# Block sums moved later, the keys' running sum queued behind the key's low part, transposed tiles in PSUM, a split query pass

## The chip, the cores and the metric

The kernel runs on one core of a Trainium2 chip. The metric is device time in microseconds for one whole execution, all inputs and outputs in device memory. Engines named below: TensorE (PE in the profile; PEld is its weight load), VectorE (DVE), ScalarE (ACT), GpSimd (POOL), SyncE (SP), which issues every DMA of this kernel. Each engine works through its own instructions strictly in the order in which the program lists them.

## The reference

Two kinds of layer alternate, A, B, A, B, on a sequence of 2048 tokens of width 512, all in fp32:

```python
def A(x):                                   # 32 heads of 16
    q, k, v = split(layernorm(x) @ wqkv)
    phi = lambda t: where(t > 0, t + 1, exp(t)) + 1e-6
    kv  = einsum("shd,she->hde", phi(k), v);  z = sum_s phi(k)
    o   = einsum("qhd,hde->qhe", phi(q), kv) / (einsum("qhd,hd->qh", phi(q), z) + 1e-6)
    return x + o @ wo
def B(x):                                   # 896 + 896 features
    z  = gelu(layernorm(x) @ w_in);  z1, z2 = z[:, :896], layernorm(z[:, 896:])
    return x + (z1 * (w_sp @ z2 + b_sp)) @ w_out      # w_sp is 2048 x 2048
```

## The kernel before

Tokens are worked in 16 tiles of 128 (NT = 16). Every large product is made of three fp32r matmuls (`mm3`): each operand is written as a high part (ScalarE copy, `high`, line 119) and a low remainder (VectorE subtraction, `low`, line 122), and high x high, high x low, low x high are added up in one PSUM bank. The third matmul (line 135) needs the low part of its first operand, the second (line 134) that of its second. Scratch memory is handed out from first-in-first-out lists: 22 `pages` of 128x512, 6 `quads`, 4 `bigs`, and the 8 PSUM `banks`. Whoever takes a slot waits until its last user is done. The order of all instructions is written out by hand.

One round (L = 0, 1) is one A layer and one B layer, in three stages:

**P1** (keys, queries). `P1.run` has steps s = 1..17. A step makes `T_high(s)`/`T_low(s)` (high and low part of the transposed, normalised tile s), `K(s-1)` and its feature map `K_phi`, `Q(s-1)` and `Q_phi` (only for the first 10 tiles), `xsplit`, `K_split(s-1)` (ScalarE line 340, VectorE line 341, then GpSimd adds the keys to their running sum `zacc`, line 346), and `Gmm(s-2)`, which accumulates x^T phi(k) in four banks. Its second matmul needs the low part from line 341. The transposition goes through memory: ScalarE writes the normalised tile, SyncE stores and reloads it, VectorE transposes 32x32 blocks (line 260, class `Turn`). The pass over `win2`, the weight of the second half of B's first product, is split into its two parts one piece at a time (`side`), from step 7 on. A step with `Q` holds 36 matmuls, a later one 24.

**P2** and `transition` before it. The last six query tiles (`later`) are projected late: one in P1's last step, three in `transition` and two in P2's steps 1 and 2 (`late`); `late_phi` then applies phi: ScalarE lines 327 and 328 (relu, exp), VectorE line 329. P2's step s has `c(s-1)` (attention output, 12 matmuls), `c2` (residual add line 614 and statistics on VectorE, then three small GpSimd instructions, lines 200 to 203), `b_high`/`b_low` (parts of the turned query tile, which `c` of the next step needs), `c3` (normalise on ScalarE, store), `d_high`/`d_low` (parts of the turned tile, which `e` needs), `e(s-3)`, `e2`, `e3` (second half of B's first product, gelu, statistics) and up to two `f` (first half).

**P4** (the 2048 x 2048 product). It is one level of a Strassen-like scheme of seven products over blocks of w_sp, in the order P2, P1, P6, P7, P4, P5, P3 (names of products here, not of stages), eight steps each, g = 0..55. The sums of blocks that P6, P7, P5 and P3 need (s[2], s[3], s[1], s[4]) are made once, by class `Sums`, during round L = 0: a `tick` stores the last sums, loads three blocks or one, and has GpSimd add two pairs (line 782). 32 ticks have work and the 33rd only stores. Step g of P4 does `fetch(g+4)` (loads the operand), `sp(g+2)` (splits it, lines 840, 841, and z, lines 870 to 874), `mm(g)` and, after a product, `evac` with the `gate` multiplications on GpSimd (line 929). After P4 comes the output product `o(i)` for 16 tiles, 21 matmuls each, with `zsplit(i+2)` ahead; in it `join` prepares the next round's P1: at i = 8 and 10 the loads of the key and query weight, at i = 10..13 their splitting, at 14 and 15 the first two turned tiles.

In the kernel before, the ticks are spread so: four in P1 of round 0 (steps 2 to 5, on sheets cut out of two `bigs` by class `Sheets`), 13 in P2 (steps 6 to 18), 16 in P4 (g = 0..15).

Of the kernel before, what the change touches and what calls it, by code (L numbers as in the profile page):

```python
# [29 lines left out]
class Slots:  # L30


    def __init__(self, pool, prefix, n):
        self.pool, self.prefix = pool, prefix
        self.free_list = deque(range(n))
        self.held = {}
        self.count = 0
# [12 lines left out]
            self.free_list.append(n)  # L50


class Sheets:


    def __init__(self, slots, n):
        self.slots = slots
        self.tiles = [slots.get([P, NF, 512]) for _ in range(n)]
        self.free_list = deque(t[:, f, :] for t in self.tiles for f in range(NF))

    def get(self, shape):
        return self.free_list.popleft()

    def put(self, *sheets):
        self.free_list.extend(sheets)

    def close(self):
        self.slots.put(*self.tiles)


@with_exitstack
def mixer_kernel(ctx: ExitStack, tc: tile.TileContext, x_in, wqkv, wo_d, win1_d, win2_d, wsp_d, bsp_d, wout_d,
                 ident_d, mask_d, out_d):
# [39 lines left out]
    def load(ap, slots=pages):  # L113
        t = slots.get(PAGE)
        nc.sync.dma_start(t, ap)
        return t

    def high(h, src):
        nc.scalar.activation(h, src, AF.Copy)  # L119
# [104 lines left out]
    class Turn:  # L224

        def __init__(self, name, by_pe, always=False):
            self.name, self.by_pe, self.always = name, by_pe, always
            self.held, self.d, self.raw = {}, {}, {}  # L230

        def turned(self, i):
# [18 lines left out]
        def get(self, i):  # L251
            if i in self.held:
                s = self.held.pop(i)
                b = transposes(s)
                if self.always:
                    pages.put(s)
                return b, banks
            r = self.raw.pop(i)
            y = pages.get([P, 4, P])
            nc.vector.transpose(y.rearrange("p c (t m) -> p m c t", m=4), r.rearrange("p (m c j) -> p m c j", m=4, c=4))  # L260
            pages.put(r)
            return y, pages


    class P1:
        def __init__(self, L):
            self.L = L
            self.st = 2 * L
            self.x, self.ms, self.xT, self.pk, self.kb, self.r, self.xhl = {}, {}, {}, {}, {}, {}, {}
            self.wk, self.wq = w_square(wqkv, 512), w_square(wqkv, 0, True)  # L270
            self.win2 = w_in2()
            self.later = deque(range(NT - DEFER, NT))
            self.turn = Turn(f"xt{L}", range(3) if L == 0 else ())
            self.G = None
            self.zacc = None

        def loadx(self, i):
            if i < NT:
# [45 lines left out]
            self.kb[i] = self.proj(i, self.wk)  # L324

        def phi(self, b, r):
            nc.scalar.activation(r, b, AF.Relu, scale=-1.0)  # L327
            nc.scalar.activation(r, r, AF.Exp, scale=-1.0)  # L328
            nc.vector.scalar_tensor_tensor(r, b, 0.0, r, op0=OP.max, op1=OP.add)  # L329
            banks.put(b)  # L330

# [5 lines left out]
        def K_split(self, i):  # L337
            r = self.r.pop(i)
            h, l = pages.get(PAGE, F32R), pages.get(PAGE, F32R)
            nc.scalar.activation(h, r, AF.Copy, bias=PHI_EPS)  # L340
            nc.vector.scalar_tensor_tensor(l, r, PHI_EPS, h.bitcast(F32), op0=OP.add, op1=OP.subtract)  # L341
            self.pk[i] = (h, l)
            if i == 0:
                self.zacc = r
            else:
                nc.gpsimd.tensor_tensor(self.zacc, self.zacc, r, op=OP.add)
                pages.put(r)

        def Q(self, i):
# [14 lines left out]
                    self.wq.free()  # L364

        def late_phi(self):
            if self.later:
                self.Q_phi(self.later.popleft())

        def xsplit(self, i):  # L370
            h, l = pages.get(PAGE, F32R), pages.get(PAGE, F32R)
# [57 lines left out]
        def run(self, sums):  # L429
            side = deque([self.win2] * NF)  # L430
            ND = NT - DEFER
            for s in range(1, NT + 2):
                self.loadx(s + 3)
                self.turn.load(s + 1)
                if 2 <= s < NT:
                    self.T_high(s)
                if s == 1:
                    if not self.kb:
                        self.K(0)
                    self.K(1)  # L440
                elif 2 < s <= NT:
                    self.K(s - 1)
                self.ln_a(s + 2)
                if 2 <= s < NT:
                    self.T_low(s)
                if s <= NT:
                    self.K_phi(s - 1)
                if s <= ND:
                    self.Q(s - 1)
                if s == NT + 1:  # L450
                    self.late()
                if s <= NT:
                    self.xsplit(s - 1)
                    self.K_split(s - 1)
                self.ln_b(s + 2)
                if s <= ND:
                    self.Q_phi(s - 1)
                if s >= 2:
                    self.Gmm(s - 2)
                if s == NT + 1:  # L460
                    self.late_phi()
                if self.L == 0 and s == 2:
                    sums.slots = Sheets(bigs, 2)
                if self.L == 0 and 2 <= s < 6:
                    sums.tick(s < 5)
                if self.L == 0 and s == 6:
                    sums.store()
                    sums.slots.close()
                    sums.slots = pages
                if s == 6:  # L470
                    self.wv, self.wo = (quads.get([P, 4, 512]) for _ in range(2))
                    nc.sync.dma_start(self.wv, wqkv[:, 1024:1536].rearrange("(c p) f -> p c f", p=P))
                    nc.sync.dma_start(self.wo, wo_d.rearrange("(c p) f -> p c f", p=P))
                if s > 6 and side:
                    side.popleft().piece()
                if s > 5 and side:
                    side[0].fetch()


    def transition(p1, p2):  # L480
# [55 lines left out]
        p1.late()  # L536
        p2.a(3)
        p2.a2(2)
        p1.late_phi()


    class P2:
# [152 lines left out]
        def run(self, sums):  # L695
            w1 = self.win1
            for s in range(1, NT + 3):
                self.loadx(s + 1)
                self.qturn.load(s + 1)
                if s in self.qturn.by_pe:  # L700
                    self.c(s - 1)
                    self.b_high(s)
                    self.c2(s - 1)
                    self.b_low(s)
                    if s >= 2:
                        self.d_high(s - 2)
                        self.d_low(s - 2)
                    self.p1.late()
                    self.c3(s - 1)
                    self.a2(s + 2)  # L710
                    self.p1.late_phi()
                    self.a(s + 3)
                else:
                    if s < NT:
                        self.b_high(s)
                    self.a2_den(s + 2)
                    if s < NT:
                        self.b_low(s)
                    if s <= NT:
                        self.c(s - 1)  # L720
                        self.c2(s - 1)
                    if s == NT:
                        quads.put(*self.W2)
                        pages.put(self.zbc)
                    self.a2_mul(s + 2)
                    late = s - 2 in self.xturn.by_pe
                    if late:
                        self.d_high(s - 2)
                        self.d_low(s - 2)
                    if s <= NT:  # L730
                        self.c3(s - 1)
                    self.a(s + 3)
                    if s <= NT + 1 and not late:
                        self.d_high(s - 2)
                        self.d_low(s - 2)
                if s >= 4:
                    self.e4(s - 4)
                self.xturn.load(s - 1)
                if s >= 3:
                    self.e(s - 3)  # L740
                    self.e2(s - 3)
                    self.e3(s - 3)
                self.f()
                self.f()
                self.fq.extend(self.fnext)
                self.fnext = []
                w1.piece(True)
                w1.fetch()
                if s > 5:
                    sums.tick()  # L750
                if s >= NT + 1:
                    self.p4.fetch(s - NT - 1)
            self.e4(NT - 1)
            self.win2.free()
# [51 lines left out]
    class P4:  # L806
# [197 lines left out]
        def run(self, nxt):  # L1004
# [10 lines left out]
            for g in range(n):  # L1015
# [6 lines left out]
                if evac_first:  # L1022
                    self.evac(p)
                    self.sp(g + 2)
                if g < 16:
                    self.sums.tick()
                if g == 3:
                    self.loadb()
# [21 lines left out]
        def join(self, i, nxt):  # L1050
# [10 lines left out]
                nxt.turn.load(i - 11)  # L1061
            if 10 <= i < 14:
                nxt.wk.piece()
                nxt.wq.piece()
            if i == 14:
                nxt.T(0)
# [48 lines left out]
```

## Time and profile before

| what | value |
|---|---|
| device time, median of 3 runs | 1405.52 us (1405.52 to 1405.92) |
| the profiled execution's own time | 1404.73 us |
| its span, first to last instruction | 1402.9 us |
| granted TensorE clock | 1.000 |
| busy: PE, DVE, ACT, POOL | 1389.6, 886.4, 561.0, 405.6 us |
| DMA traffic | 225.69 MB, 161 GB/s on average |

A row of the views has the start and the duration (us) or, for groups, the count and the mean duration of one instruction (ns); in brackets stands how long the engine was idle before it and what ended that. "pg", "qd", "bg", "bank" are the four kinds of slots; "x<-y" means that x is written from y. A matmul's end is modelled, so that the busy time of TensorE overlaps: what counts is the distance from one start to the next.

### The profile page before, as it was taken

What the parts mean: (1) busy time and instruction counts of PE and PEld (TensorE: products, weight loads), DVE (VectorE), ACT (ScalarE), POOL (GpSimd) and SP (SyncE); (2) the same over time, 40 slices, a digit from 0 to 9 for tenths busy, and PEclk for the clock granted to TensorE, in tenths of its full rate; (3) what the DMA queues carried; (4) which work ended last, traced back from release to release, by engine and by line L of the source; (5) the groups of instructions that cost most, each with busy time, mean ns of one, the idle gap of its engine ahead of it and who ended that gap; (6) DMA issues with size and microseconds to landing.
All of it is one profiled execution on the core that took longest, in us unless ns stands there. A gap on an engine that the chain in (4) does not pass through costs nothing.

```text
span 1402.9 us, 17320 instructions
## 1 busy us (share of the span) xinstructions
PE 1389.6 (99%) x6230; PEld 1156.7 (82%) x6230; DVE 886.4 (63%) x1251; ACT 561.0 (40%) x847; POOL 405.6 (29%) x490
## 2 busy tenths in 40 slices
PE   9999999999999999999999999999999999999998
PEld 7877788888888888888788778888888888888887
DVE  7786777752577666573577867766415466665632
ACT  5564534434323332341356645444333233333420
POOL 4644345544365002040023434432100030022300
PEclk9999999999999999999999999999999999999999
DMA  5842267876897433443635413555334344334432
GB/s 176 270 142 62 73 192 237 271 228 207 305 326 248 134 120 135 173 158 120 210 101 184 129 46 99 179 179 162 114 116 158 104 165 134 133 117 167 155 110 94
DMA packets 142263, 225.69 MB, mean 161 GB/s; under 512 B 11744, under 2 KB 50400, under 8 KB 142176
## 3 DMA queue, kind: packets, MB, share of 16 engines
q1 hardware_dynamic: 142176, 224.57, 48.6%
q8 instruction: 49, 0.80, 0.2%
q14 instruction: 38, 0.31, 0.1%
HBM read 156.63 MB, written 67.90 MB: 160 GB/s over the span
## 4 chain that ended last, share of the span: by engine, by line
PE 87%; DVE 6%; ACT 4%; issue 1%; DMA 1%; POOL 0%; SPq 0%; DVEq 0%; ACTq 0%; POOLq 0%
PE bank L135 15%; PE bank L134 15%; PE bank L133 15%; PE bank L902 13%; PE bank L904 13%; PE bank L903 13%; DVE pg L260 1%; DVE pg L341 1%; DVE pg L329 1%; ACT pg L328 1%; DMA pg<-in_win_dram 1%; ACT pg L327 1%; PE bank L515 1%; PE bank L526 0%; PE bank L221 0%
## 5 line engine op out<-in xcount | busy, mean ns | idle before, releaser
L902 PE MATMUL bank<-qd,pg 128*128 128x512 f32 x800 | 311.2, 389 | 0.0
L904 PE MATMUL bank<-qd,pg 128*128 128x512 f32 x800 | 311.2, 389 | 0.0
L903 PE MATMUL bank<-qd,pg 128*128 128x512 f32 x800 | 311.2, 389 | 0.0
L841 DVE TENSOR_TENSOR qd<-qd,qd 128x1024 fp32r<-128x1024 f32 x112 | 151.8, 1355 | 178.7 <-ACT qd L840 174.2
L840 ACT ACTIVATE qd<-qd 128x1024 fp32r<-128x1024 f32 x112 | 118.5, 1058 | 215.7 <-PE bank L904 199.0
L929 POOL TENSOR_TENSOR bg<-bg,pg 128x512 f32<-128x512 f32 x56 | 85.5, 1564 | 409.7 <-DVE bg L956 195.5
L904 PEld LDWEIGHTS bank<-qd,pg 128*128 128x128 f32 x800 | 150.2, 188 | 31.3
L903 PEld LDWEIGHTS bank<-qd,pg 128*128 128x128 f32 x800 | 150.2, 188 | 31.2
L902 PEld LDWEIGHTS bank<-qd,pg 128*128 128x128 f32 x800 | 150.1, 188 | 31.1
L135 PE MATMUL bank<-qd,pg 128*128 128x512 f32 x384 | 150.7, 392 | 2.5 <-DVE pg L122 2.5
L200 POOL TENSOR_SCALAR rs<-mv 128x1 f32<-128x1 f32 x96 | 36.4, 379 | 384.4 <-DVE mv L198 377.2
L209 ACT ACTIVATE pg<-pg,nb,rs 128x512 f32<-128x512 f32 x63 | 51.1, 811 | 181.6 <-POOL nb L203 175.5
L133 PE MATMUL bank<-qd,pg 128*128 128x512 f32 x288 | 112.4, 390 | 0.0
L134 PE MATMUL bank<-qd,pg 128*128 128x512 f32 x288 | 112.3, 390 | 0.0
L782 POOL TENSOR_TENSOR pg<-pg,pg 128x512 f32<-128x512 f32 x56 | 81.5, 1456 | 47.7 <-DMA pg<-in_wsp_dram 41.8
L133 PE MATMUL bank<-bg,qd 128*128 128x448 f32 x256 | 94.1, 368 | 0.0
L135 PE MATMUL bank<-bg,qd 128*128 128x448 f32 x256 | 93.7, 366 | 0.1
L134 PE MATMUL bank<-bg,qd 128*128 128x448 f32 x256 | 93.6, 366 | 0.0
L135 PEld LDWEIGHTS bank<-qd,pg 128*128 128x128 f32 x384 | 72.0, 188 | 20.8 <-DVE pg L122 6.0
L135 PE MATMUL bank<-wo,qd 128*128 128x512 f32 x224 | 87.3, 390 | 0.8 <-DVE qd L122 0.8
L133 PE MATMUL bank<-wo,qd 128*128 128x512 f32 x224 | 87.3, 390 | 0.7 <-ACT qd L119 0.7
L135 PE MATMUL bank<-qd,bg 128*128 128x512 f32 x224 | 87.4, 390 | 0.0
(121 smaller groups left out, 2571.7 us busy)
## 6 DMA issues: line engine op xcount, KB each, us to landing
qd<-s SPq DMA_DIRECT2D x64, 512.0 KB, 3.4
qd<-in_wsp_dram SPq DMA_DIRECT2D x48, 512.0 KB, 3.8
pg<-x SPq DMA_DIRECT2D x64, 256.0 KB, 2.9
z<-pg SPq DMA_DIRECT2D x56, 256.0 KB, 2.5
pg<-in_wsp_dram SPq DMA_DIRECT2D x56, 256.0 KB, 5.0
s<-pg SPq DMA_DIRECT2D x56, 256.0 KB, 4.8
pg<-z SPq DMA_DIRECT2D x56, 256.0 KB, 5.4
x<-pg SPq DMA_DIRECT2D x48, 256.0 KB, 2.6
```

The costliest lines, as they stand in the source:

```text
L133: nc.tensor.matmul(out, ah, bh, start=start, stop=False)
L134: nc.tensor.matmul(out, ah, bl, start=False, stop=False)
L135: nc.tensor.matmul(out, al, bh, start=False, stop=stop)
L200: nc.gpsimd.tensor_scalar(rs, mv[:, 1:2], LN_EPS, None, op0=OP.add)
L209: nc.scalar.activation(y, x, AF.Identity, bias=nb, scale=rs)
L782: nc.gpsimd.tensor_tensor(t, a, b, op=OP.add)
L840: nc.scalar.activation(w[:, 0], r, AF.Copy)
L841: nc.vector.tensor_sub(w[:, 1], r, w[:, 0].bitcast(F32))
L902: m(out, h[:, o], w[:, 0, j, :], start=start, stop=False, skip_group_check=True)
L903: m(out, h[:, o], w[:, 1, j, :], start=False, stop=False, skip_group_check=True)
L904: m(out, l[:, o], w[:, 0, j, :], start=False, stop=stop, skip_group_check=True)
L929: nc.gpsimd.tensor_tensor(u, u, z1, op=OP.mult)
```

## The change

Seven edits:

1. Class `Sheets` and P1's ticks go. The ticks now run from P2's step 5 (14 of them, one more than before) to P4's g = 18 (19, three more); all their blocks lie in pages.
2. `win2` is split from P1's step 4 on (loaded from step 3 on), instead of step 7 (6).
3. `behind`: GpSimd's add to `zacc` (line 346) waits for the VectorE instruction of line 341 in the same `K_split`.
4. P1's reloaded tiles are transposed into a PSUM bank instead of a page (`inbank`); lines 119 and 122 then read the bank.
5. `late_phi` is cut in two. For the last call in `transition` and those in P2, the ScalarE half stays where it was, and the VectorE half (line 329) goes behind `c2` of the next step, ahead of `b_low`.
6. In `join` the query weight is split at i = 11..14 instead of 10..13.
7. P4's `tick` bound goes from g < 16 to g < 19 (with edit 1).

```diff
--- before.py
+++ after.py
@@ -50,24 +50,6 @@
             self.free_list.append(n)
 
 
-class Sheets:
-
-
-    def __init__(self, slots, n):
-        self.slots = slots
-        self.tiles = [slots.get([P, NF, 512]) for _ in range(n)]
-        self.free_list = deque(t[:, f, :] for t in self.tiles for f in range(NF))
-
-    def get(self, shape):
-        return self.free_list.popleft()
-
-    def put(self, *sheets):
-        self.free_list.extend(sheets)
-
-    def close(self):
-        self.slots.put(*self.tiles)
-
-
 @with_exitstack
 def mixer_kernel(ctx: ExitStack, tc: tile.TileContext, x_in, wqkv, wo_d, win1_d, win2_d, wsp_d, bsp_d, wout_d,
                  ident_d, mask_d, out_d):
@@ -114,6 +96,11 @@
         t = slots.get(PAGE)
         nc.sync.dma_start(t, ap)
         return t
+
+    def behind(ins, other):
+
+        tc.add_manual_dep(ins.ins, other.ins.name, mybir.DependencyInfo(
+            mybir.DependencyClass.Sync, mybir.DependencyReason.DATA))
 
     def high(h, src):
         nc.scalar.activation(h, src, AF.Copy)
@@ -225,8 +212,8 @@
 
 
 
-        def __init__(self, name, by_pe, always=False):
-            self.name, self.by_pe, self.always = name, by_pe, always
+        def __init__(self, name, by_pe, always=False, inbank=False):
+            self.name, self.by_pe, self.always, self.inbank = name, by_pe, always, inbank
             self.held, self.d, self.raw = {}, {}, {}
 
         def turned(self, i):
@@ -256,10 +243,11 @@
                     pages.put(s)
                 return b, banks
             r = self.raw.pop(i)
-            y = pages.get([P, 4, P])
+            home = banks if self.inbank else pages
+            y = home.get([P, 4, P])
             nc.vector.transpose(y.rearrange("p c (t m) -> p m c t", m=4), r.rearrange("p (m c j) -> p m c j", m=4, c=4))
             pages.put(r)
-            return y, pages
+            return y, home
 
 
     class P1:
@@ -270,9 +258,10 @@
             self.wk, self.wq = w_square(wqkv, 512), w_square(wqkv, 0, True)
             self.win2 = w_in2()
             self.later = deque(range(NT - DEFER, NT))
-            self.turn = Turn(f"xt{L}", range(3) if L == 0 else ())
+            self.turn = Turn(f"xt{L}", range(3) if L == 0 else (), False, True)
             self.G = None
             self.zacc = None
+            self.half = None
 
         def loadx(self, i):
             if i < NT:
@@ -324,8 +313,14 @@
             self.kb[i] = self.proj(i, self.wk)
 
         def phi(self, b, r):
+            self.phi_a(b, r)
+            self.phi_b(b, r)
+
+        def phi_a(self, b, r):
             nc.scalar.activation(r, b, AF.Relu, scale=-1.0)
             nc.scalar.activation(r, r, AF.Exp, scale=-1.0)
+
+        def phi_b(self, b, r):
             nc.vector.scalar_tensor_tensor(r, b, 0.0, r, op0=OP.max, op1=OP.add)
             banks.put(b)
 
@@ -338,12 +333,12 @@
             r = self.r.pop(i)
             h, l = pages.get(PAGE, F32R), pages.get(PAGE, F32R)
             nc.scalar.activation(h, r, AF.Copy, bias=PHI_EPS)
-            nc.vector.scalar_tensor_tensor(l, r, PHI_EPS, h.bitcast(F32), op0=OP.add, op1=OP.subtract)
+            last = nc.vector.scalar_tensor_tensor(l, r, PHI_EPS, h.bitcast(F32), op0=OP.add, op1=OP.subtract)
             self.pk[i] = (h, l)
             if i == 0:
                 self.zacc = r
             else:
-                nc.gpsimd.tensor_tensor(self.zacc, self.zacc, r, op=OP.add)
+                behind(nc.gpsimd.tensor_tensor(self.zacc, self.zacc, r, op=OP.add), last)
                 pages.put(r)
 
         def Q(self, i):
@@ -364,8 +359,18 @@
                     self.wq.free()
 
         def late_phi(self):
+            self.late_phi_a()
+            self.late_phi_b()
+
+        def late_phi_a(self):
             if self.later:
-                self.Q_phi(self.later.popleft())
+                self.half = self.qb, ztag(self.later.popleft(), PAGE, f"q{self.L}")
+                self.phi_a(*self.half)
+
+        def late_phi_b(self):
+            if self.half is not None:
+                self.phi_b(*self.half)
+                self.half = None
 
         def xsplit(self, i):
             h, l = pages.get(PAGE, F32R), pages.get(PAGE, F32R)
@@ -459,21 +464,13 @@
                     self.Gmm(s - 2)
                 if s == NT + 1:
                     self.late_phi()
-                if self.L == 0 and s == 2:
-                    sums.slots = Sheets(bigs, 2)
-                if self.L == 0 and 2 <= s < 6:
-                    sums.tick(s < 5)
-                if self.L == 0 and s == 6:
-                    sums.store()
-                    sums.slots.close()
-                    sums.slots = pages
                 if s == 6:
                     self.wv, self.wo = (quads.get([P, 4, 512]) for _ in range(2))
                     nc.sync.dma_start(self.wv, wqkv[:, 1024:1536].rearrange("(c p) f -> p c f", p=P))
                     nc.sync.dma_start(self.wo, wo_d.rearrange("(c p) f -> p c f", p=P))
-                if s > 6 and side:
+                if s > 3 and side:
                     side.popleft().piece()
-                if s > 5 and side:
+                if s > 2 and side:
                     side[0].fetch()
 
 
@@ -536,7 +533,7 @@
         p1.late()
         p2.a(3)
         p2.a2(2)
-        p1.late_phi()
+        p1.late_phi_a()
 
 
     class P2:
@@ -701,6 +698,7 @@
                     self.c(s - 1)
                     self.b_high(s)
                     self.c2(s - 1)
+                    self.p1.late_phi_b()
                     self.b_low(s)
                     if s >= 2:
                         self.d_high(s - 2)
@@ -708,7 +706,7 @@
                     self.p1.late()
                     self.c3(s - 1)
                     self.a2(s + 2)
-                    self.p1.late_phi()
+                    self.p1.late_phi_a()
                     self.a(s + 3)
                 else:
                     if s < NT:
@@ -746,7 +744,7 @@
                 self.fnext = []
                 w1.piece(True)
                 w1.fetch()
-                if s > 5:
+                if s > 4:
                     sums.tick()
                 if s >= NT + 1:
                     self.p4.fetch(s - NT - 1)
@@ -1022,7 +1020,7 @@
                 if evac_first:
                     self.evac(p)
                     self.sp(g + 2)
-                if g < 16:
+                if g < 19:
                     self.sums.tick()
                 if g == 3:
                     self.loadb()
@@ -1061,6 +1059,7 @@
                 nxt.turn.load(i - 11)
             if 10 <= i < 14:
                 nxt.wk.piece()
+            if 11 <= i < 15:
                 nxt.wq.piece()
             if i == 14:
                 nxt.T(0)
```

## The prediction

> **What bounds the kernel now.** I read the page's head first, then who waits for whom on TensorE, then the single stalls in the timeline.
>
> ```profile
> PE 1389.6 (99%) x6230; PEld 1156.7 (82%) x6230; DVE 886.4 (63%) x1251; ACT 561.0 (40%) x847; POOL 405.6 (29%) x490
> PE bank L134 <- DVE pg L341: 3.2, 5, 0.7
> PE bank L135 <- DVE pg L122: 2.5, 4, 0.7
> PE bank L135 <- DVE qd L122: 0.8, 1, 0.8
> PE bank L133 <- ACT qd L119: 0.7, 1, 0.7
> 102.26 0.39 PE L135 MATMUL bank<-qd,pg 128*128 128x512 f32 x1
> 102.49 0.39 PE L133 MATMUL bank<-pg,pg 128*128 128x512 f32 x1
> 103.53 0.50 PE L134 MATMUL bank<-pg,pg 128*128 128x512 f32 x1 [0.65 <-DVE pg L341]
> 103.86 0.39 PE L135 MATMUL bank<-pg,pg 128*128 128x512 f32 x1
> ```
>
> TensorE is the bound, and no edit touches a matmul. What can be won is only its stalls. The four wait rows hold 7.2 us in 11 waits (us, times, longest). One stall costs more than its idle time, because the busy time overlaps: matmuls follow each other every 0.23 us (102.26 to 102.49), but here the next steps are 1.04 and 0.33 us, so 0.81 + 0.10 = 0.91 us for a wait shown as 0.65. With that 0.27 us more per wait, the 11 waits are worth 7.2 + 11 x 0.27 = **10.2 us**. The smallest unit that a measurement of this kernel can tell from no change is about 0.2%, 2.8 us.
>
> By place: five waits on line 341 in P1 are 3.2 + 1.35 = 4.6 us (three in round 0, two in round 1); four on line 122 after the transition are 2.5 + 1.1 = 3.6 us (two in each round); the last two rows, in `join`, are 0.8 + 0.7 + 0.5 = 2.0 us.
>
> **P1 (edits 2, 3, 4): 4.6 us.** The chain that ended last shows P1's step 12 as one serial loop:
>
> ```profile
> 97.62 1.03 DVE pg L260
> 98.67 0.63 ACT z_h L119
> 99.82 0.64 ACT pg L328
> 100.48 0.70 DVE pg L329
> 101.21 0.64 ACT pg L340
> 101.87 1.61 DVE pg L341
> 103.52 0.56 DVE bg L122
> 104.08 1.03 DVE pg L260
> L341 DVE SCALAR_TENSOR_TENSOR pg<-pg,pg x32: 691/1601/1773, 18.9 to 820.1; 128x512 fp32r<-128x512 f32 x32
> L346 POOL TENSOR_TENSOR pg<-pg,pg x30: 1291/1662/1676, 24.1 to 819.5; 128x512 f32<-128x512 f32 x30
> ```
>
> The loop is 104.08 - 97.62 = 6.46 us long; TensorE needs 24 x 0.227 = 5.44 us for such a step, so it runs dry once its lead is used up. Two pieces leave the loop. The piece of `win2` (line 122 into "bg", 0.56) falls into steps 4 to 10 instead, where a step has 36 matmuls (8.16 us) and the loop, with one more line 329 for `Q`, is 6.46 + 0.69 = 7.15 us; its ScalarE part and its load move along. And line 341 is 1.6 us long only where GpSimd's line 346 runs beside it: the row's minimum is 0.69, its median 1.60. `behind` starts line 346 when line 341 has ended. Loop after: 6.46 - 0.56 - 0.91 = **4.99 us**, below 5.44, so all five waits go.
>
> What `behind` makes late: on GpSimd only the next step's three small statistics instructions stand behind line 346 in P1. Line 346 would start 0.7 us later, but without line 341 beside it and with its 1.3 us minimum it ends about when it does now. Its last sum is needed by the transition only after the first late query pass. Cost nil.
>
> At this place the Trainium skill speaks, "SBUF — State Buffer", section "SBUF: two separate sides": a VectorE instruction with two SBUF inputs and a GpSimd instruction share one port pair, the first to start holds it and the other blocks fully. Line 341's minimum of 0.69 and median of 1.60 us agree. By that page line 346, now second, would in its turn block the next VectorE instruction with two SBUF inputs.
>
> In the loop's order the next is the transposition (one input), then the low part of the turned tile, which edit 4 makes read a bank; in steps 4 to 10 it is the piece of `win2`, where 1.0 us a step is to spare. So I take no cost, and keep the other end as a rival.
>
> Edit 4 changes line 260's target. No VectorE row here writes PSUM. Its reads of PSUM cost nothing extra (line 329, 0.70 us). Bounds: a gain down to such a 0.70 us instruction (-0.3), or a doubled transposition (+1.0). I take 0, the row itself, since the number of elements is the same; the slack for it is 5.44 - 4.99 = 0.45 us a step. Each step now takes one more bank, three of the four that `G` leaves free in steps with `Q`; each is released a step before its turn comes again, so no wait.
>
> **The transition (edit 5): 3.6 us.**
>
> ```profile
> 150.87 0.69 DVE L329 SCALAR_TENSOR_TENSOR z_q<-bank,z_q 128x512 f32<-128x512 f32 x1 [1.91 <-ACT z_q L328]
> 151.48 0.68 DVE L614 TENSOR_TENSOR pg<-pg,bank 128x512 f32<-128x512 f32 x1
> 153.01 0.66 DVE L122 TENSOR_TENSOR pg<-bank,pg 128x512 fp32r<-128x512 f32 x1
> 150.74 0.58 ACT L119 ACTIVATE pg<-bank 128x512 fp32r<-128x512 f32 x1
> 149.00 0.39 PE L135 MATMUL bank<-qd,pg 128*128 128x512 f32 x1
> 153.73 0.50 PE L135 MATMUL bank<-qd,pg 128*128 128x512 f32 x1 [0.70 <-DVE pg L122]
> ```
>
> VectorE stands idle 1.91 us for the ScalarE half of a late query tile, with the residual add and statistics of `c2` queued behind it, whose matmuls are done by 149.4. After: line 614 at 149.5, the statistics (which now fill 152.2 to 153.0) to 151.0, line 329 at 151.1 (ScalarE was done at 150.8), `b_low` 151.7 to 152.4. TensorE asks for it where it would stand without a stall, at 153.73 less the idle 0.70 and the 0.16 of overlap, 152.87: 0.5 us to spare. Step 2 is alike, with more to spare since `c3` also starts earlier. All four waits go.
>
> **`join` (edit 6): 2.0 us.**
>
> ```profile
> 689.15 0.63 ACT L119 ACTIVATE qd<-pg 128x512 fp32r<-128x512 f32 x1 [6.93 <-DMA pg<-in_wqkv_dram]
> 689.68 0.93 ACT L119 ACTIVATE qd<-bg 128x896 fp32r<-128x896 f32 x1
> ```
>
> ScalarE waits 6.93 us for the query weight, loaded in the same step, and `zsplit(13)` (689.68) queues behind. One step later `zsplit(13)` and the key piece go first; the query piece may wait until 689.15 as now, and `zsplit(14)` after it must be ready only one output tile later (21 x 0.227 = 4.8 us). Step 14 gets the last piece (0.6 ScalarE, 0.7 VectorE), where `zsplit` has run out. Both waits go.
>
> **The sums (edits 1, 7): +1.3 us.** P1 of round 0 loses four ticks, which hid under steps without a stall: nothing to win. The cost is at the two new ends.
>
> ```profile
> 203.17 0.96 SPq L115 DMA_DIRECT2D pg<-in_wsp_dram  x2
> 208.83 2.66 POOL L782 TENSOR_TENSOR pg<-pg,pg 128x512 f32<-128x512 f32 x2 [3.49 <-DMA pg<-in_wsp_dram]
> 191.60 1.55 SPq L115 DMA_DIRECT2D pg<-in_win_dram  x1
> 196.93 0.56 POOL L200 TENSOR_SCALAR rs<-mv 128x1 f32<-128x1 f32 x1 [2.61 <-DVE mv L198]
> 199.91 0.69 DVE L122 TENSOR_TENSOR qd<-pg,qd 128x512 fp32r<-128x512 f32 x1 [1.50 <-ACT qd L119]
> 201.91 0.36 PE L135 MATMUL bank<-bg,qd 128*128 128x448 f32 x1
> 172.20 1.15 DVE L196 BATCH_NORM_STATS2 st<-z_z 128x6 f32<-128x448 f32 x2 [0.33 <-ACT z_z L667]
> ```
>
> P2's first tick has nothing preloaded: its adds start 208.83 - 203.17 = 5.66 us after its loads are issued, and the statistics behind them on GpSimd wait. At step 5 the loads go out at about 193.2 (after the row at 191.60), the adds run 198.9 to 201.5, and line 200 of 196.93 moves to 201.5: 4.6 us later. `d_low` of tile 4 follows: 200.6 + 4.6 = 205.2, asked for by TensorE at 201.91. Edit 5 lets this chain start earlier, three times by up to 1.9 us, of which 1.7 is lost again as TensorE too is earlier; but the gelu statistics (172.20) hold it by step 4, so I count 1.7 us of gain. Stall 205.2 - 1.7 - 201.9 = 1.6 us, between 0 and 3.3. Less a stall of 0.3 us that stands in that stretch now, I take +1.3.
>
> The other end is P4's P6. Its last operand, s[2] of block 7, is stored by the tick of g = 18 and loaded at g = 19.
>
> ```profile
> 441.21 12.66 POOL L929 TENSOR_TENSOR bg<-bg,pg 128x512 f32<-128x512 f32 x8 [8.45 <-DVE bg L939]
> L782 POOL TENSOR_TENSOR pg<-pg,pg 128x512 f32<-128x512 f32 x56 | 81.5, 1456 | 47.7 <-DMA pg<-in_wsp_dram 41.8
> s<-pg SPq DMA_DIRECT2D x56, 256.0 KB, 4.8
> qd<-s SPq DMA_DIRECT2D x64, 512.0 KB, 3.4
> 463.58 1.06 ACT L840 ACTIVATE qd<-qd 128x1024 fp32r<-128x1024 f32 x1 [2.61 <-PE bank L904]
> 471.54 0.39 PE L902 MATMUL bank<-qd,pg 128*128 128x512 f32 x1
> ```
>
> The adds of g = 16 and 17 queue behind the eight gates, done at 453.9: four adds of 1.46 end at 459.7, store 4.8, load 3.4: there at 467.9, and 1.06 (ScalarE) + 1.2 (VectorE) make 470.2. The matmuls start at 471.54. So 1.3 us to spare, cost 0, and every microsecond beyond is lost. SyncE's `fetch` of steps 22 to 24 queues behind those stores.
>
> **Sum.** 1404.73 - 4.6 - 3.6 - 2.0 + 1.3 = 1395.8 us for the profiled execution; the median lies 0.8 above that (1405.52 against 1404.73): **1396.6 us**.
>
> **Rivals.** *All stalls go and P2 absorbs the tick* (bound 0): 1395.3; *P2 at its other bound* (+3.3): 1398.6. Both belong to the forecast's own range, 1394 to 1399, chance 0.62.
>
> *The wait in P1 moves and stays.* Line 346 blocks the next two-input instruction, or the transposition into PSUM is dearer: with +0.9 in the loop it is 5.9 us again and P1's 4.6 us are not won: 1401.2. That rule of the Trainium skill (same page and section) would give this where such an instruction follows. For it: nearly every row of line 341 is contended now (median 1.60). Against: the order above. Chance 0.12.
>
> *The change does less than it says*, as the 0.5 us to spare at `b_low` or the 1.3 us in P6 are used up by a few tenths to 4 us: about 1400. Chance 0.10.
>
> *Slower: GpSimd's gates and the sums' pages lock each other in P4.* Around g = 15 the 22 pages are nearly all taken (8 for z1, 4 for the bias, the sums' blocks, the splits of z), so splits and loads get pages that the gates release one by one. If `sp(18)` must wait for the whole run of gates (453.9 + 2.8 = 456.7 where its matmuls start at 451.1) 5.6 us are lost, and if the last blocks are also loaded only then, the last sum comes 7.5 us too late as well: 1396.6 + 13.1 = 1409.7. It decides from the point where a split waits over 8 us. For it: the pages are counted in the code, and the gates took 12.66 us. Against: the gates release in turn, each 1.58 us, and splits run two steps (8 us) ahead. Chance 0.10; 0.06 is left for stalls that I don't see, of either size.
>
> **How the numbers follow.** Forecast and the two part-way rivals are faster by over 0.2%: 0.62 + 0.12 + 0.10, less 0.02 for their tails: 0.82. Slower: 0.10 + 0.04 of the rest = 0.14. Same: 0.04. The range goes from all stalls gone with a little more (1394.0) to just beyond the P1 rival (1402.0).
>
> **What would show it.** Line 341 at a median of 0.69 us in its row, no wait of TensorE on line 341; no wait on line 122 near 152 and 160 (and 848, 855); ScalarE's wait for the query weight still there, but no TensorE wait behind it; line 782's first wait at about 195 with a TensorE stall of about 1.6 us near 200; no stall before P6's last step. Wrong: line 260 over 1.5 us, line 122 or 329 stretched to 1.6 us in line 341's place, or TensorE waiting on line 840 or 870 in P4.

## The result

| | kernel before | changed kernel |
|---|---|---|
| median | 1405.52 us (4 runs, 1405.23 to 1405.92) | 1393.79 us (4 runs, 1393.02 to 1394.11) |
| profiled execution, its span | 1404.73, 1402.9 us | 1393.49, 1391.6 us |

The ratio is 0.9916, 95% interval 0.9898 to 0.9933: faster by 11.7 us where 8.9 were forecast. The median lies 0.2 us below the stated range (1394.0 to 1402.0); two of the four runs, 1394.09 and 1394.11 us, lie inside it. A second set of runs of the changed kernel, described below, gave 1393.36 us and 0.9913 (0.9900 to 0.9927).

In the changed kernel the lines are shifted: 336 is what was 341 (key's low part), 341 was 346 (key sum), 248 was 260 (transposition), 106 and 109 were 119 and 122 (high, low), 120 to 122 were 133 to 135 (the three matmuls), 324 was 329, 611 was 614, 185 and 187 were 198 and 200, 97 was 115 (the loads), 780 was 782, 838 was 840.

From the page, the busy time, share and instructions of each engine; then the whole view of who waits for whom on TensorE (us, times, longest):

```profile
PE 1385.0 (100%) x6230; PEld 1158.6 (83%) x6230; DVE 853.8 (61%) x1251; ACT 562.1 (40%) x847; POOL 387.7 (28%) x490
```

```profile
PE bank L412 <- DVE pg L407: 2.3, 1, 2.3
PE bank L120 <- ACT qd L106: 0.5, 1, 0.5
```

The eleven waits that stood in the four rows before are gone. What is left is the wait at the very start, which the kernel before has too, and one new one of 0.5 us.

**Where the 11.4 us of span came from** (1402.95 less 1391.57). The view of waits shows only idle time, so I summed for every matmul of both traces the distance from its start to the next start, less 0.2267 us, the distance when nothing holds it up (0.200 for 448 columns, 0.109 for 128): the time by which TensorE was late, whether or not it counts as idle.

| place | late before, us | after | won | forecast |
|---|---|---|---|---|
| P1, both rounds | 3.6 + 2.4 | 0 | 6.0 | 4.6 |
| behind the transition, both rounds | 1.94 + 2.04 | 0.10 + 0.19 | 3.7 | 3.6 |
| output product and start of the next P1 | 1.99 + 0.29 | 0 | 2.3 | 2.0 |
| P2 of round 0 | 1.04 | 1.62 | -0.6 | -1.3 |
| all | 22.3 | 11.0 | 11.4 | 8.9 |

The rest of the lateness is the same in both (start, plain fp32 matmuls, changes of shape).

**P1.** Groups of VectorE instructions by line, with their shapes (busy us, mean ns, idle before), then VectorE's timeline in one of the short steps:

```profile
L336 DVE SCALAR_TENSOR_TENSOR pg<-pg,pg 128x512 fp32r<-128x512 f32 x32 | 22.2, 692 | 3.3 <-ACT pg L335 0.3
L248 DVE STREAM_TRANSPOSE bank<-pg 128x512 f32<-128x512 f32 x29 | 20.9, 720 | 1.6 <-DMA pg<-xt 1.6
L248 DVE STREAM_TRANSPOSE pg<-pg 128x512 f32<-128x512 f32 x46 | 49.2, 1070 | 3.2 <-DMA pg<-yt 3.2
```

```profile
100.43 0.72 DVE L248 STREAM_TRANSPOSE bank<-pg 128x512 f32<-128x512 f32 x1
103.87 0.69 DVE L324 SCALAR_TENSOR_TENSOR pg<-bank,pg 128x512 f32<-128x512 f32 x1 [1.36 <-ACT pg L321]
105.26 0.69 DVE L336 SCALAR_TENSOR_TENSOR pg<-pg,pg 128x512 fp32r<-128x512 f32 x1
105.87 0.72 DVE L248 STREAM_TRANSPOSE bank<-pg 128x512 f32<-128x512 f32 x1
```

The key's low part takes 0.69 us in every step, as forecast, and GpSimd's key sum, no longer beside it, 1.29 us (median; 1.66 before). The transposition into the bank takes 0.72 us where the one into a page takes 1.07. From one transposition to the next are 5.44 us, TensorE's own time for the step, and VectorE now waits for ScalarE, which waits for the matmuls: the loop follows TensorE.

**Behind the transition** (VectorE, and the matmul that needs the result):

```profile
145.88 0.69 DVE L611 TENSOR_TENSOR pg<-pg,bank 128x512 f32<-128x512 f32 x1 [0.47 <-PE bank L122]
147.44 0.66 DVE L324 SCALAR_TENSOR_TENSOR z_q<-bank,z_q 128x512 f32<-128x512 f32 x1
148.01 0.68 DVE L109 TENSOR_TENSOR pg<-bank,pg 128x512 fp32r<-128x512 f32 x1
149.32 0.39 PE L122 MATMUL bank<-qd,pg 128*128 128x512 f32 x1
```

The idle time in front of `c2` fell from 1.91 (before line 329) to 0.47 us, and `b_low` ends at 148.69, 0.63 us ahead of need (0.5 forecast).

**The first tick in P2** (SyncE, GpSimd, then TensorE):

```profile
185.85 2.95 SPq L97 DMA_DIRECT2D pg<-in_wsp_dram  x4
191.37 2.66 POOL L780 TENSOR_TENSOR pg<-pg,pg 128x512 f32<-128x512 f32 x2 [3.25 <-DMA pg<-in_wsp_dram]
194.13 0.23 POOL L187 TENSOR_SCALAR rs<-mv 128x1 f32<-128x1 f32 x1
195.90 0.39 PE L122 MATMUL bank<-qd,pg 128*128 128x512 f32 x1
196.78 0.47 PE L120 MATMUL bank<-bg,qd 128*128 128x448 f32 x1 [0.50 <-ACT qd L106]
```

The adds wait 5.5 us from the issue of their loads (5.66 forecast), the statistics stand behind them, and TensorE loses 1.1 us in all here (starts 0.66 + 0.11 + 0.22 + 0.11 late). In exchange 0.55 us of lateness that P2 had before near 215 and 238 is gone.

**The end of the sums in P4** cost nothing. ScalarE's split of P6's last operand:

```profile
460.93 1.06 ACT L838 ACTIVATE qd<-qd 128x1024 fp32r<-128x1024 f32 x1 [2.54 <-DMA qd<-s]
```

The matmuls that use it start at 466.73, two steps later, so after ScalarE's 2.54 us of waiting 5.8 us were left; ScalarE's and VectorE's parts take 1.06 + 1.2, and about 3.5 us were to spare instead of the 1.3 forecast. GpSimd's last adds end at 456.34, so the store and the load took 4.6 us together, where the prediction had 4.8 + 3.4.

### The profile page after: what moved, and what is told of

Same layout as the page of the kernel before. It is cut to its first block, busy times and chain, and to the rows that moved or that the text cites. A ratio compares the mean times of both kernels' runs of the same rounds, so it can differ in the third digit from the quotient of the medians.

```text
span 1391.6 us, 17297 instructions
## 1 busy us (share of the span) xinstructions
PE 1385.0 (100%) x6230; PEld 1158.6 (83%) x6230; DVE 853.8 (61%) x1251; ACT 562.1 (40%) x847; POOL 387.7 (28%) x490
## 4 chain that ended last, share of the span: by engine, by line
PE 96%; DVE 2%; ACT 1%; POOL 1%; issue 0%; DMA 0%; POOLq 0%; DVEq 0%; ACTq 0%
PE bank L122 18%; PE bank L121 18%; PE bank L120 18%; PE bank L902 13%; PE bank L901 13%; PE bank L900 13%; PE bank L512 1%; PE bank L523 0%; PE bank L208 0%; DVE st L183 0%; PE bank L412 0%; DMA pg<-in_wsp_dram 0%; POOL rs L188 0%; DVE pg L109 0%; ACT pg L196 0%
## 5 line engine op out<-in xcount | busy, mean ns | idle before, releaser
L900 PEld LDWEIGHTS bank<-qd,pg 128*128 128x128 f32 x800 | 150.1, 188 | 31.4
L901 PEld LDWEIGHTS bank<-qd,pg 128*128 128x128 f32 x800 | 150.2, 188 | 31.2
L902 PEld LDWEIGHTS bank<-qd,pg 128*128 128x128 f32 x800 | 150.2, 188 | 31.0
L187 POOL TENSOR_SCALAR rs<-mv 128x1 f32<-128x1 f32 x96 | 27.2, 284 | 352.5 <-DVE mv L185 351.8
L780 POOL TENSOR_TENSOR pg<-pg,pg 128x512 f32<-128x512 f32 x64 | 94.2, 1472 | 50.7 <-DMA pg<-in_wsp_dram 27.9
L122 PE MATMUL bank<-qd,bg 128*128 128x512 f32 x224 | 87.5, 390 | 0.0
L121 PE MATMUL bank<-qd,bg 128*128 128x512 f32 x224 | 87.4, 390 | 0.0
L120 PE MATMUL bank<-qd,bg 128*128 128x512 f32 x224 | 87.2, 389 | 0.0
L120 PE MATMUL bank<-wo,qd 128*128 128x512 f32 x224 | 87.1, 389 | 0.0
```

The source lines that it names most:

```text
L120: nc.tensor.matmul(out, ah, bh, start=start, stop=False)
L121: nc.tensor.matmul(out, ah, bl, start=False, stop=False)
L122: nc.tensor.matmul(out, al, bh, start=False, stop=stop)
L187: nc.gpsimd.tensor_scalar(rs, mv[:, 1:2], LN_EPS, None, op0=OP.add)
L780: nc.gpsimd.tensor_tensor(t, a, b, op=OP.add)
L900: m(out, h[:, o], w[:, 0, j, :], start=start, stop=False, skip_group_check=True)
```

## The experiments

All start from the changed kernel. The first six runs take P1 apart. The undone and partial versions were timed once each, and whole spans of one kernel scatter (the kernel before: 1402.4 to 1405.2 us in nine runs), so the argument goes by TensorE's lateness at its place.

**All three P1 edits undone.**

```diff
-  range(3) if L == 0 else (), False, True)
+  range(3) if L == 0 else ())
-  behind(nc.gpsimd.tensor_tensor(self.zacc, self.zacc, r, op=OP.add), last)
+  nc.gpsimd.tensor_tensor(self.zacc, self.zacc, r, op=OP.add)
-  if s > 3 and side:  ...  if s > 2 and side:
+  if s > 6 and side:  ...  if s > 5 and side:
```

> Edits 2, 3 and 4 undone (win2 split from step 7, key sum not held behind the key's low part, turned tiles in pages); the sums stay moved. Theory (P1's stalls come from the serial loop, and short stalls are missing in the view of waits): the loop is 6.46 us again, TensorE loses 6.0 us more in P1 than in the changed kernel (3.6 in round 0, 2.4 in round 1), span 1391.6 + 6.0 = 1397.6. Rival (the block sums' transfers and GpSimd adds, which left P1 of round 0, caused the stalls there): only round 1 loses, 2.4 us, span 1394.0. Second rival (the wait view's 4.6 us was the whole worth): 1396.2.

Measured: span 1397.0 us, time 1398.77. Waits of TensorE (the second row is the stall near 196 us that the changed kernel has too):

```profile
PE bank L121 <- DVE pg L336: 3.0, 5, 0.7
PE bank L120 <- ACT qd L106: 0.6, 1, 0.6
```

Five waits on the key's low part come back, shown as 3.0 us, while TensorE is 5.2 us late in P1 (2.76 and 2.45): the view shows a little more than half. That supports the loop, and that the sum from the wait rows was too low. Round 0 lost 2.76 us and not 3.6: with this loop, the block sums in P1 of the kernel before cost 0.8 us there, so the first rival holds for a small part (how, the run with the sums put back shows below). Also the 0.29 us at the start of the next P1 came back.

**Each P1 edit undone alone** (the edits above, one at a time).

> Edit 3 alone undone: the key sum on GpSimd starts beside line 336 again. Theory (the loop, now about 4.6 us against 5.44 of TensorE, has slack for one edit): the loop gets 0.9 longer, 5.5, about TensorE's own 5.44: loss under 0.5 us, span 1391.6 to 1392.1. Rival (the three edits' worths add up, by their shares 0.91, 0.56, 0.36 of the loop): 3.0 us of P1's 6.0 come back, span 1394.6.

> Edit 4 alone undone: turned tiles in pages. Theory (slack): the transposition takes 1.08 us again instead of 0.72, loop about 5.0 us, no loss, span 1391.6. Rival (adding up): 1.2 us come back, span 1392.8. Second rival: the key sum on GpSimd, held behind line 336, now blocks the low part of the turned tile, which again has two inputs in SBUF (0.69 to 1.2 us or more), and P1 loses 1 to 3 us.

Without `behind`: span 1392.3 us, no lateness in P1, though line 336 is back at 1544 ns (the 0.7 us of span were lost at the start and near 196 us). With turned tiles in pages: 1392.0 us, no lateness in P1 either; only the 0.29 us at the start of the next P1 returned, so that gain belongs to the transposition. In both, the loop keeps up; the shares don't add up. The key sum did not slow the low part of the turned tile (693 ns), which the second rival had expected.

> Edit 2 alone undone: win2 split from step 7 on. Theory (slack): loop 4.6 + 0.56 = 5.2 us, below 5.44, no loss, span 1391.6. Rival (adding up): 1.8 us come back, span 1393.4.

Span 1394.9 us, time 1396.68: both were wrong, the cost is 2.74 us in P1 (1.39 and 1.35). Another 0.44 us was lost near 23 us, before this edit can act; that spot is late by 0 to 0.4 us from run to run. The group of the `win2` piece, and one instance of it with GpSimd's key sum:

```profile
L109 DVE TENSOR_TENSOR bg<-pg,bg 128x512 fp32r<-128x512 f32 x14 | 13.8, 986 | 3.6 <-ACT bg L106 3.6
```

```profile
101.27 0.69 DVE L336 SCALAR_TENSOR_TENSOR pg<-pg,pg 128x512 fp32r<-128x512 f32 x1
102.04 1.29 POOL L341 TENSOR_TENSOR pg<-pg,pg 128x512 f32<-128x512 f32 x1 [1.80 <-DVE pg L336]
102.49 1.39 DVE L109 TENSOR_TENSOR bg<-pg,bg 128x512 fp32r<-128x512 f32 x1 [0.53 <-ACT bg L106]
103.80 0.72 DVE L248 STREAM_TRANSPOSE bank<-pg 128x512 f32<-128x512 f32 x1
```

In the changed kernel this group's mean is 684 ns. Here the piece starts at 102.49, while the key sum runs until 103.33, and ends 0.55 us after it: the wait that `behind` took from line 336 went to the next VectorE instruction with two inputs in pages or bigs. That is the rival "the wait moves and stays" of the prediction, which the order in the changed kernel avoids.

**One P1 edit alone.**

> Of the three edits in P1 only edit 3 (key sum held behind the key's low part); edits 2 and 4 undone. Theory (the port is only passed on): the piece of win2, which follows in the short steps, waits for the key sum instead of line 336: line 336 at 0.69 us, line 109 into bg at 1.4 us in steps 11 to 13, loop 6.4 us, P1 loses as much as with all three undone (5.2 us) less at most 1 us, span 1396 to 1397. Rival (the hold is worth its 0.91 us wherever it stands): loop 5.55 us, P1 loses at most 1.5 us, span 1391.6 to 1393.1.

Span 1396.5 us: P1 4.7 us late (2.34 and 2.37), the theory. TensorE now waits for the turned tile instead of the key's low part (view of waits), and the piece of `win2` has a mean of 986 ns, the same group row as above:

```profile
PE bank L120 <- ACT z_h L106: 2.2, 4, 0.8
```

> Of the three edits in P1 only edit 2 (win2 split from step 4 on); edits 3 and 4 undone. Theory (loop without the piece of win2: 6.46 - 0.56 = 5.9 us against 5.44, but TensorE enters the short steps with a lead of about 1 us or more): P1 loses 0 to 1.5 us against the changed kernel, span 1391.6 to 1393.1. Rival (any loop over 5.44 us brings the stalls back from the second short step on, five steps of 0.46 us a round): 3 to 4.5 us, span 1394.6 to 1396.

Span 1393.8 us; P1 is 1.94 us late (0.97 a round), a little over the theory's bound and well under the rival's; the remaining 0.29 is again the start of the next P1. So of the 5.2 us, edit 2 alone wins 3.3, `behind` alone 0.5, and with edit 2 either of the other two wins the rest. The bank alone was not run.

**The late query pass back in one piece** (edit 5 undone: `late_phi()` at the three places, no `late_phi_b`).

> Edit 5 undone: both halves of the late query pass where they were. Theory: the four stalls behind the transition come back, 1.85 us a round, 3.7 in all, and the stall near 196 us grows by up to 1.7 us since P2's chain starts later: span 1395.3 to 1397.0. Rival (the chain's lead does not reach step 5, the gelu statistics hold it): 3.7 us and no growth near 196, span 1395.3.

Span 1396.0 us; the view of waits shows the old row again (the first one; the second is the stall near 196 us):

```profile
PE bank L122 <- DVE pg L109: 2.5, 4, 0.7
PE bank L120 <- ACT qd L106: 1.0, 1, 1.0
```

3.7 us come back behind the transition. The lateness near 196 us is 1.64 us, against 0.9 to 1.5 in the versions that keep the edit and begin the ticks as the changed kernel does: at most 0.7 us of the head start of 1.7 us that the prediction counted for P2's chain shows.

**Query weight split one tile earlier** (edit 6 undone).

```diff
-  if 11 <= i < 15:
       nxt.wq.piece()
```

> Edit 6 undone: query weight split one output tile earlier. Theory: the two stalls in the output product come back, 2.0 us, span 1393.6; the 0.29 us at the start of the next P1 stays away, since the quicker transposition into the bank removed it. Rival: that 0.29 us came from the same delay and comes back too, span 1393.9.

Span 1393.4 us; 1.38 us come back in the output product (2.0 expected: the first of the two stalls is 0.29 us here instead of 0.94; why was not followed up), and the 0.29 us at the start of the next P1 stays away, as the theory said.

**Sums where they were** (edits 1 and 7 undone).

```diff
-  if s > 4:  sums.tick()      ...  if g < 19:
+  if s > 5:  sums.tick()      ...  if g < 16:
+  four ticks in P1's steps 2 to 5, on Sheets(bigs, 2)
```

> Edits 1 and 7 undone (four ticks in P1 of round 0 on sheets of two bigs, 13 in P2, 16 in P4), the rest as in the changed kernel. Theory (moving the sums brought nothing but the stall at P2's first tick): the 1.1 us near 196 go, the smaller stalls of the kernel before near 215 and 238 (0.55 us) may come back, no stall in P1: span 1390.5 to 1391.1. Rival (the sums in P1 of round 0 hold back its loop): 1 to 3.6 us more in P1, span 1392 to 1395. Third possibility: the later end of the sums had a cost in P4 that is too small to see, then no difference there.

Span 1391.1, one time of 1392.83 us. P2 loses its 1.1 us of lateness (the 0.53 left stand in every version), and the old stalls near 215 and 238 don't come back. P1 has one stall, 0.55 us at 72, against the theory (lines are shifted by 18 here: 124 and 127 are 106 and 109, 138 and 140 are 120 and 122):

```profile
69.22 0.63 ACT L124 ACTIVATE bg<-pg 128x512 fp32r<-128x512 f32 x1 [3.84 <-DMA pg<-in_win_dram]
72.05 0.39 PE L140 MATMUL bank<-pg,pg 128*128 128x512 f32 x1
72.71 0.50 PE L138 MATMUL bank<-qd,pg 128*128 128x512 f32 x1 [0.28 <-DVE pg L127]
```

ScalarE waits 3.84 us for the load of a piece of `win2`, and the parts of the next turned tile stand behind it. The kernel before has the same wait, 3.88 us at 67.66; with the sums moved away and P1 otherwise as before (all three P1 edits undone) it is 0.40 us. So the ticks did hold P1 of round 0 back: by 0.55 us here, through this load, and by 0.8 us with the old loop; that the same wait accounts for all of the 0.8 was not tested.

Taken together, in the changed kernel the move of the sums costs about 0.5 us by the traces; the time of a single run can't settle so little.

**First blocks loaded a step ahead.**

```diff
+  if s == 4:
+      sums.fetch()
   if s > 4:
       sums.tick()
```

> The changed kernel with the first three blocks of the sums loaded one step before the first tick in P2 (step 4). Theory (the one stall left near 196 us, 1.1 us, is GpSimd waiting for those loads with the statistics queued behind): the stall goes or shrinks under 0.3 us, span 1390.5 to 1390.8, ratio to the kernel before 0.9907. Rival (the tick's two adds themselves, 2.7 us on GpSimd at this step, hold the statistics): the stall stays at 0.6 to 1.1 us, span 1391.0 to 1391.6. Second rival (the load one step earlier fills the queue of SyncE or takes pages): a new stall near 185 us, span over 1391.6.

Median of four runs 1392.52 us (1392.05 to 1393.58), ratio 0.9904 (0.9888 to 0.9921). GpSimd goes on to the adds without a wait, and TensorE's only wait is the one at the start (782 is 780 in the changed kernel):

```profile
188.20 2.99 POOL L782 TENSOR_TENSOR pg<-pg,pg 128x512 f32<-128x512 f32 x2
191.68 0.56 POOL L187 TENSOR_SCALAR rs<-mv 128x1 f32<-128x1 f32 x1 [0.48 <-DVE mv L185]
```

```profile
PE bank L412 <- DVE pg L407: 2.3, 1, 2.3
```

The span of this execution was 1391.8 us, against the theory's 1390.8 at most: the lateness near 196 is gone (1.62 to 0.53 for P2), and VectorE's last instruction ends at 1387.69 us instead of 1388.57, but from there to the end of the span pass 4.1 us instead of 3.0; why is open. This version and the changed kernel were timed again on one chip.

> The changed kernel once more, timed beside the version with preloaded sums on one chip. Expected: 1393.8 us, ratio to the kernel before 0.9916, one stall near 196 us of about 1.1 us.

> The version with the first blocks of the sums loaded one step ahead, timed beside the changed kernel on one chip. Theory: 1.1 us less than the changed kernel's run of the same call, 1392.6 us, no TensorE wait behind the start. Rival: the difference seen before lay in the scatter between calls, and the two medians lie within 0.3 us.

Changed kernel 1393.36 us (1393.14 to 1393.61), with preload 1392.74 (1392.02 to 1393.19); spans 1391.7 and 1390.7 us, clock 1.000 both; VectorE's last instruction ends at 1388.67 and 1387.68 us. All lateness sums agree within 0.15 us but P2's: 1.44 and 0.53. The preloading version is ahead by 0.6 us in the medians and 1.0 in the spans; the intervals against the kernel before, 0.9900 to 0.9927 and 0.9894 to 0.9921, overlap. The 0.6 us lie between the theory's 1.1 and the rival's 0.3, so the trace shows the gain and the times alone don't prove it.

## Why the prediction was right and where it was wrong

**Right in mechanism, in the main.** TensorE was the bound, and its stalls were what was won: lateness and span both fell by 11.4 us. The loop in P1 no longer holds TensorE up, the four stalls behind the transition went with 0.6 us to spare, ScalarE's wait for the query weight stayed but hid, P2's first tick made a new stall, and P4 had slack. In P1 the shares of the edits were not as forecast: the prediction had `behind` take 0.91 of the 1.47 us out of the loop, but `behind` alone won 0.5 of 5.2 us and edit 2 alone 3.3, and with edits 2 and 4 in place P1 is not late without `behind`.

**Wrong in size, by 2.8 us, mainly in four terms.**

1. *The sum of the stalls, "7.2 + 11 x 0.27 = 10.2 us".* It was 12.0 (6.0 + 3.7 + 2.3). The rows of the view count idle time alone. Here the shown ends of matmuls overlap by 0.16 us, so that TensorE can be late without being idle: late starts of 0.23 us (at 122.28) and 0.27 us (at 817.72) are not in the rows. In P1 such starts made up the missing 1.4 us (0.34 near 122, 0.38 near 817, about 0.1 each near 97, 113 and 809, the rest in hundredths). P1 was worth 6.0 us and not 4.6. Start-to-start distances show that. By cause, 5.2 of the 6.0 us come back with the three P1 edits undone; the other 0.8 belongs to the sums.
2. *The sums, "+1.3".* In P2 it was +0.6: a stall of 1.1 instead of 1.6, less 0.55 instead of 0.3. The prediction placed the loads 1.5 us behind the load before them (the row at 191.60), but that one now took 0.42 us, and the loads went out earlier; and the statistics lost 2.4 us (191.7 with the blocks there, 194.1 without), not 4.6. At most 0.7 of the head start of 1.7 us that it set against this shows. These are two errors of opposite sign, so that the stall came out only 0.5 us too large is in part luck. In P1 the prediction put the four ticks at nothing, since they "hid under steps without a stall"; with them a load of `win2` came late, and their going is the 0.8 us above.
3. *`join`, 2.0.* It was 2.3: the 0.29 us at the start of the next P1, also missing in the wait rows, went too, through the transposition into the bank. The prediction took 0 for that edit's own worth, with a gain of 0.3 us an instruction as the bound; 0.35 is what it is.
4. *The offset of the median from the profiled execution, 0.8.* It was 0.3. The first three terms and 0.1 for the transition bring the forecast to 1396.6 - 1.4 - 0.7 - 0.3 - 0.1 = 1394.1, just inside the range; this last half microsecond, which is scatter between executions, takes it out.

**The step that failed** is the first: what the stalls are worth was taken from the wait rows, 10.2 us, and the range's lower end, "all stalls gone with a little more", with it. The start-to-start distances give 12.0 us; with them, and the old 0.55 us in P2 gone, the lower end would have been 1405.5 - 12.0 - 0.5 = 1393.0.

**Rivals.** "The wait moves and stays" did not happen, but it is real: without edit 2 it cost 2.7 us. The Trainium skill ("SBUF — State Buffer", "SBUF: two separate sides") states that of a VectorE instruction with two SBUF inputs and a GpSimd instruction that reads SBUF the first to start holds the shared port pair and the other blocks. The trace agrees: line 109, started 0.45 us into GpSimd's add, took 1.39 us and ended 0.55 us after it. The lock of gates and pages in P4 didn't occur: with the sums' adds done at 456.3, ScalarE had the operand by 460.93, and TensorE is no later in P4 than before.

## What to carry to other kernels

Where one engine is busy all the time, measure its lateness by start-to-start distances, not by idle time: here late starts of at most 0.3 us each, which are not in the view of waits, were a quarter of P1's worth. Moving a contending instruction behind its victim only helps if what follows the victim does not contend too; look at the next instruction in the queue before moving. And where a batch of work is started later, load its first blocks one step ahead, or the first batch stands in the queue in front of others' work.

## What the hardware showed that was not expected

VectorE's 32x32 block transposition of 128x512 fp32 took 720 ns into a PSUM bank (mean of 29 in the changed kernel) and 1070 to 1077 ns into SBUF (mean of 46 there and of 75 in the kernel before), from the same kind of source; both write with a stride of four elements. GpSimd is not the reason: with the turned tiles in pages, 22 of the transpositions into SBUF ran with no GpSimd instruction beside them and took 1068 to 1094 ns. Reading the result from the bank was no dearer either (line 109: 679 ns from a bank, 693 from a page in the run with turned tiles in pages; line 106: 0.60 and 0.63 us).
